# Moving an SSM kernel's skip term from TensorE to GpSimd, and its first loads to two DMA queues

## Chip, cores, metric

One core of one Trainium2 chip. The metric is the device time of one execution in microseconds. The profiled span (first to last instruction) is some 2 us shorter than the time.

## The reference

```python
xn = layernorm(x)                                   # x: 1 x 2048 x 512, bf16
# S5 layer: complex diagonal recurrence over 2048 steps, 512 states
h[t] = Lam_bar * h[t-1] + B_bar @ xn[t]
s = 2 * Re(C @ h) + xn * Dskip                      # the skip term is xn * Dskip
g = silu((gelu(xn @ w_gate) * (xn @ w_up)) @ w_down)    # hidden width 1376
out = x + s * g
```

## The kernel before

It works in four stages of 512 tokens. In each, TensorE does the gated FFN (`ffn`, 11 blocks), the projections for the next stage's scan (`u_pair`), the down projection of four 128-token tiles (`down`) and, in the following stage, the output product of those tiles (`y_mm`). VectorE rotates, scans and rotates back (pp, qq, Wt, Ft, hst), forms the gating products (`at`) and finishes each tile (`epi`). ScalarE empties PSUM (the memory of the tiles that TensorE writes; all these tiles share eight buffers) and applies gelu and silu. `TT` is VectorE's instruction with two inputs, `ACT` one of ScalarE. The skip term costs four small products a tile, of xnT with a diagonal matrix that holds Dskip, accumulated in the same PSUM tile:

```python
def y_mm(s, m, hst):
    ...
    for j in range(2 * NPT):
        nc.tensor.matmul(y_ps[:, :], lhsT=hst[...], rhs=C2[...], start=(j == 0), stop=False)
    for kt in range(KT):                       # the skip term
        nc.tensor.matmul(y_ps[:, kt * P : (kt + 1) * P], lhsT=xnT[:, kt, mg : mg + P],
                         rhs=diagI[:, kt, :], start=False, stop=(kt == KT - 1))

def epi(s, m, y_ps, g2):                       # yg, ot are bf16
    TT(out=yg[:], in0=y_ps[:, :], in1=g2[:], op=ALU.mult)
    TT(out=ot[:], in0=yg[:], in1=x_tok[:, s * M + m, :], op=ALU.add)
```

The loads stand on one queue (sync): four tiles of x, B_re, B_im, then the FFN weights in pieces. The tiny vectors are on the other (scalar). TensorE runs 13 products on zeros while it waits, then transposes B and xn, then starts the first projection.

Of the kernel before, what the change touches and what calls it, by code (L numbers as in the profile page):

```python
# [19 lines left out]
def kernel(  # L20
# [17 lines left out]
    nc = tc.nc  # L38
# [36 lines left out]
    wd = consts.tile([P, NFT, D], BF16, name="wd")  # L75
    BT = consts.tile([P, 2, KT, D], BF16, name="BT")
    C2 = consts.tile([P, 2, NPT, D], BF16, name="C2")
    pv = consts.tile([16, P], BF16, name="pv")
    at0 = work.tile([P, NFT, TS], BF16, name="at", tag="at")
# [7 lines left out]
    wu_r = B_w_up.rearrange("(k p) f -> p k f", p=P)  # L87
    for m in range(M):
        nc.sync.dma_start(out=x_tok[:, m, :], in_=x_r[:, m, :])
    for i, v in enumerate((A_log_dt, A_Lambda_im, A_Lambda_re, A_Dskip)):  # L90
        nc.scalar.dma_start(out=pv[4 * i : 4 * i + 4, :], in_=v.rearrange("(k p) -> k p", p=P))
    for ri, src in enumerate((A_B_re, A_B_im)):
        nc.sync.dma_start(out=Bn[:, ri, :, :], in_=src.rearrange("(k p) d -> p k d", p=P))
    cuts = [0, 3 * P, 7 * P, F]
    for i, (a, b) in enumerate(zip(cuts[:-1], cuts[1:])):
        nc.sync.dma_start(out=wg[:, :, a:b], in_=wg_r[:, :, a:b])
        nc.sync.dma_start(out=wu[:, :, a:b], in_=wu_r[:, :, a:b])
        if i == 0:
            nc.sync.dma_start(out=x_tok[:, M : 2 * M, :], in_=x_r[:, M : 2 * M, :])
# [73 lines left out]

    pf = consts.tile([P, 16], FP32, name="pf")
    ldt, lim, lre, dsk = (pf[:, 4 * i : 4 * i + 4] for i in range(4))
    dt_, thn, a1, rho = (small(n) for n in ("dt_", "thn", "a1", "rho"))
# [6 lines left out]

    dummies(10)
    pt_ps = psum.tile([P, 16], BF16, name="pt_ps", tag="ps")
    nc.tensor.transpose(pt_ps[:, :], pv[:, :], ident[0:16, 0:16])
    dummies(3)
    bn(0, 0)
    bn(0, 1)
    bn_end(0, 0)  # L190
    bn_end(0, 1)
    rstd(0, 0, 2)
    bn(0, 2)
    nc.vector.tensor_copy(out=pf[:], in_=pt_ps[:, :])
    nc.gpsimd.tensor_tensor(out=dt_[:], in0=euler[:], in1=ldt, op=ALU.pow)
    bn(0, 3)
    bn_end(0, 2)
    bn_end(0, 3)
    rstd(0, 2, 4)
    xs = [norm0(0), norm0(1)]  # L200
    STT(out=thn[:], in0=lim, scalar=1.0 / (2.0 * math.pi), in1=dt_[:], op0=ALU.mult, op1=ALU.mult)
    TT(out=a1[:], in0=lre, in1=dt_[:], op=ALU.mult)
    nc.gpsimd.tensor_tensor(out=rho[:], in0=euler[:], in1=a1[:], op=ALU.pow)
    b_transposes(0)
    tps = [t_xn0(0, xs[0]), t_xn0(1, xs[1])]
    xs += [norm0(2), norm0(3)]
    b_transposes(1)
    for m in range(2):
        nc.vector.tensor_copy(out=xnT[:, :, m * P : (m + 1) * P], in_=tps[m][:, :, :])
    tps += [t_xn0(2, xs[2]), t_xn0(3, xs[3])]  # L210
    for m in range(2, 4):
        nc.vector.tensor_copy(out=xnT[:, :, m * P : (m + 1) * P], in_=tps[m][:, :, :])  # L212


# [26 lines left out]
    cre, cim, ncre = small("cre"), small("cim"), small("ncre")  # L241
    diagI = consts.tile([P, KT, P], BF16, name="diagI")

    def coefficients():
# [20 lines left out]
        TSC(out=ncre[:], in0=cre[:], scalar1=-1.0, scalar2=None, op0=ALU.mult)  # L265
        for kt in range(KT):
            TSC(out=diagI[:, kt, :], in0=ident_f[:], scalar1=dsk[:, kt : kt + 1], scalar2=None, op0=ALU.mult)

    def fold_c(pt):
        tA = work.tile([P, D], FP32, name="tA", tag="tA")  # L270
        tB = work.tile([P, D], FP32, name="tB", tag="tB")
        ACT(out=tA[:], in_=CT[:, 1, pt, :], func=AF.Copy, scale=cim[:, pt : pt + 1])
        ACT(out=tB[:], in_=CT[:, 0, pt, :], func=AF.Copy, scale=cim[:, pt : pt + 1])
        dve(now() + 0.8, 0.66, lambda: STT(
            out=C2[:, 0, pt, :], in0=CT[:, 0, pt, :], scalar=cre[:, pt : pt + 1], in1=tA[:],
            op0=ALU.mult, op1=ALU.subtract,
        ))
        dve(now() + 1.6, 0.66, lambda: STT(
            out=C2[:, 1, pt, :], in0=CT[:, 1, pt, :], scalar=ncre[:, pt : pt + 1], in1=tB[:],
            op0=ALU.mult, op1=ALU.subtract,  # L280
        ))
# [151 lines left out]
    def down(s, m, at):  # L433
# [7 lines left out]
        pe_takes(NFT)  # L441
        g2 = work.tile([P, D], FP32, name="g2", tag="g2", bufs=6)
        ACT(out=g2[:], in_=f_ps[:, :], func=AF.Silu)  # L443
        return g2

    def y_mm(s, m, hst):
        m0 = m * P
        mg = s * TS + m0
        for h in range(2):
            flush(("h", s, h))  # L450
        y_ps = psum.tile([P, D], FP32, name="y_ps", tag="ps")
        for j in range(2 * NPT):
            nc.tensor.matmul(  # L453
                y_ps[:, :], lhsT=hst[:, j // NPT, j % NPT, m0 : m0 + P], rhs=C2[:, j // NPT, j % NPT, :],
                start=(j == 0), stop=False,
            )
        for kt in range(KT):
            nc.tensor.matmul(  # L458
                y_ps[:, kt * P : (kt + 1) * P], lhsT=xnT[:, kt, mg : mg + P], rhs=diagI[:, kt, :],
                start=False, stop=(kt == KT - 1),  # L460
            )
        pe_takes(2 * NPT + 1)
        return y_ps

    def epi(s, m, y_ps, g2):
        mg = s * TS + m * P
        yg = work.tile([P, D], BF16, name="yg", tag="yg")
        ot = work.tile([P, D], BF16, name="ot", tag="ot")

        def f():  # L470
            TT(out=yg[:], in0=y_ps[:, :], in1=g2[:], op=ALU.mult)  # L471
            TT(out=ot[:], in0=yg[:], in1=x_tok[:, s * M + m, :], op=ALU.add)

        dve(now() + 0.3, 0.95, f)
        nc.sync.dma_start(out=out_td[mg : mg + P, :], in_=ot[:])

    def y_halves(s, m, hst, g2):
        m0 = m * P
        mg = s * TS + m0
        yg = work.tile([P, D], BF16, name="yg", tag="yg")  # L480
        ot = work.tile([P, D], BF16, name="ot", tag="ot")
        for i in range(2):
            c = slice(i * D // 2, (i + 1) * D // 2)
            y_ps = psum.tile([P, D // 2], FP32, name="y_ps", tag="ps")
            for j in range(2 * NPT):
                nc.tensor.matmul(
                    y_ps[:, :], lhsT=hst[:, j // NPT, j % NPT, m0 : m0 + P], rhs=C2[:, j // NPT, j % NPT, c],
                    start=(j == 0), stop=False,
                )
            for kt in range(KT // 2):  # L490
                k = i * (KT // 2) + kt
                nc.tensor.matmul(
                    y_ps[:, kt * P : (kt + 1) * P], lhsT=xnT[:, k, mg : mg + P], rhs=diagI[:, k, :],
                    start=False, stop=(kt == KT // 2 - 1),
                )
            TT(out=yg[:, c], in0=y_ps[:, :], in1=g2[:, c], op=ALU.mult)
            TT(out=ot[:, c], in0=yg[:, c], in1=x_tok[:, s * M + m, c], op=ALU.add)
            (nc.sync, nc.scalar)[i].dma_start(out=out_td[mg : mg + P, c], in_=ot[:, c])
# [22 lines left out]
    def ln_out(s, m):  # L521
# [3 lines left out]
        nc.sync.dma_start_transpose(out=xnT[:, :, c0 : c0 + P], in_=xn[:])  # L525


    for ri, src in enumerate((A_C_re, A_C_im)):
# [4 lines left out]

    clk["pe"] = 9.5
    clk["dve"] = 11.0
# [91 lines left out]
```

## Time and profile before

| | before |
|---|---|
| time | 189.46 us median of 3 (188.73 to 190.42) |
| span of the profiled run | 187.6 us |
| TensorE, VectorE, GpSimd busy | 96%, 83%, 11% |
| first projection starts | 10.35 us |
| last scan result (hst of stage 3) written | 157.4 us |
| first product on it | 166.6 us |

The busy shares and slices are in the prediction below. Here are two views that it only names. The list of instructions in order of time, TensorE at the start; columns are start (us), length (us), engine, line, operation, output and inputs, shapes, count, and in brackets the idle time before and what ended it:

```profile
6.77 1.07 PE L140 MATMUL tb_ps<-ident,Bn 128*128 128x128 bf16 x16 [1.04 <-DMA Bn<-in_A_B_re_dram]
...
10.35 1.02 PE L333 MATMUL u_ps<-xnT,BT 128*128 128x512 bf16 x4 [0.62 <-DVE xnT L212]
```

TensorE waits 1 us for B_re, then transposes, and starts the real work at 10.35 us. The waits of TensorE over the whole run; columns are who waited for whom, us in total, times, longest:

```profile
PE u_ps L333 <- DVE xnT L212: 0.6, 1, 0.6
PE u_ps L333 <- DMA xnT<-xn: 0.5, 1, 0.5
```

With the 1 us for B_re these are all its waits after the products on zeros. Two groups of VectorE, by form (busy us, mean ns, idle before):

```profile
L382 DVE TENSOR_TENSOR_SCAN Ft<-rho,it,Wt 128x512 bf16<-128x512 f32 x24 | 29.9, 1271 | 0.0
...
L431 DVE TENSOR_TENSOR at<-gt,ub 128x512 bf16<-128x512 bf16 x40 | 16.4, 414 | 5.9 <-ACT ub L430 5.8
```

### The profile page before, as it was taken

The page shows a single profiled execution, that of the slowest core. Times are in us where ns is not written, and L with a number is a line of the kernel's source. Part 1 is how long each engine was busy: PE and PEld are TensorE (multiplying, and loading weights), DVE is VectorE, ACT ScalarE, POOL GpSimd, SP SyncE. Part 2 cuts the span into 40 slices and gives each one's busy share as a digit, 9 for nine tenths or more (in the row PEclk, how much of TensorE's full clock was granted, in tenths as well). Part 3 has the DMA queues.
Part 4 walks back from the last instruction along what each step waited for, and adds up shares of the span by engine and source line. Part 5 has one row for each costly group of instructions (what it writes and reads, how often), then busy time and mean ns, then how long its engine had stood idle before and what let it go on. Part 6 is the DMA issues. An engine that isn't in the chain of part 4 may idle for free.

```text
span 187.6 us, 2592 instructions
## 1 busy us (share of the span) xinstructions
PE 180.8 (96%) x918; PEld 86.0 (46%) x918; DVE 156.0 (83%) x269; ACT 116.2 (62%) x209; POOL 21.2 (11%) x35
## 2 busy tenths in 40 slices
PE   7789999999999999999999999989999999999992
PEld 2644444444444444544444444544444444554452
DVE  4859999999999599999999997999999999332033
ACT  3499899997279969257259947937428733441210
POOL 3745400000000330000000192000000000000000
PEclk9999999999999999999999999999999999999999
DMA  5999968600000013200000001420000000000001
GB/s 145 330 365 361 225 123 246 119 3 0 0 0 0 0 30 86 56 28 28 3 2 0 2 0 42 101 56 28 0 0 0 3 0 28 28 29 31 28 28 58
DMA packets 21164, 12.26 MB, mean 65 GB/s; under 512 B 11456, under 2 KB 21152, under 8 KB 21152
## 3 DMA queue, kind: packets, MB, share of 16 engines
q1 hardware_dynamic: 20976, 12.03, 23.9%
q8 instruction: 7, 0.11, 0.2%
q10 hardware_dynamic: 176, 0.07, 0.1%
q14 instruction: 5, 0.04, 0.1%
HBM read 7.38 MB, written 2.10 MB: 51 GB/s over the span
## 4 chain that ended last, share of the span: by engine, by line
PE 57%; DVE 21%; ACT 10%; DMA 4%; POOL 3%; issue 3%; SPq 1%; POOLq 1%; ACTq 0%; DVEq 0%
PE f_ps L438 15%; PE u_ps L333 11%; PE g_ps L418 10%; PE up_ps L423 10%; PE y_ps L453 6%; DVE Ft L382 6%; ACT junk L508 3%; DVE qq L352 3%; ACT gt L428 3%; ACT ub L430 3%; DVE pp L352 3%; DVE Wt L356 2%; DMA Bn<-in_A_B_re_dram 2%; DMA xnT<-xn 2%; DVE at L431 1%
## 5 line engine op out<-in xcount | busy, mean ns | idle before, releaser
L418 PE MATMUL g_ps<-xnT,wg 128*128 128x512 bf16 (+1 forms) x176 | 45.2, 379 | 0.0
L423 PE MATMUL up_ps<-xnT,wu 128*128 128x512 bf16 (+1 forms) x176 | 45.2, 379 | 0.0
L438 PE MATMUL f_ps<-wd,at 128*128 128x512 bf16 (+1 forms) x176 | 38.7, 379 | 0.0
L428 ACT ACTIVATE gt<-g_ps 128x512 bf16<-128x512 f32 (+1 forms) x44 | 26.0, 592 | 10.0 <-PE g_ps L418 7.8
L382 DVE TENSOR_TENSOR_SCAN Ft<-rho,it,Wt 128x512 bf16<-128x512 f32 x24 | 29.9, 1271 | 0.0
L333 PE MATMUL u_ps<-xnT,BT 128*128 128x512 bf16 x128 | 28.3, 379 | 1.1 <-DVE xnT L212 0.6
L430 ACT ACTIVATE ub<-up_ps 128x512 bf16<-128x512 f32 (+1 forms) x44 | 26.3, 597 | 3.9 <-PE up_ps L423 3.8
L453 PE MATMUL y_ps<-C,hst 128*128 128x512 bf16 x120 | 28.3, 379 | 0.0
L423 PEld LDWEIGHTS <-wu 128*128 128x128 bf16 (+1 forms) x176 | 17.6, 100 | 20.4
L438 PEld LDWEIGHTS <-at 128*128 128x128 bf16 (+1 forms) x176 | 17.2, 98 | 20.6
L443 ACT ACTIVATE g<-f_ps 128x512 f32<-128x512 f32 x16 | 9.6, 597 | 27.1 <-PE f_ps L438 27.1
L418 PEld LDWEIGHTS <-wg 128*128 128x128 bf16 (+1 forms) x176 | 17.2, 100 | 18.4
L431 DVE TENSOR_TENSOR at<-gt,ub 128x512 bf16<-128x512 bf16 (+1 forms) x44 | 18.1, 414 | 7.3 <-ACT ub L430 7.1
L338 ACT ACTIVATE U<-u_ps 128x512 bf16<-128x512 f32 x32 | 17.8, 602 | 9.0 <-PE u_ps L333 9.0
L471 DVE TENSOR_TENSOR yg<-y_ps,g 128x512 bf16<-128x512 f32 x15 | 10.3, 684 | 13.7 <-PE y_ps L458 9.9
L333 PEld LDWEIGHTS <-BT 128*128 128x128 bf16 x128 | 12.3, 98 | 15.9 <-issue 1.4
L453 PEld LDWEIGHTS <-hst 128*128 128x128 bf16 x120 | 11.7, 98 | 13.6
L523 ACT ACTIVATE xn<-x_tok,nb,rs 128x512 bf16<-128x512 bf16 x12 | 9.7, 812 | 5.6 <-POOL nb L519 5.6
L513 POOL TENSOR_SCALAR sx<-sx 128x4 f32<-128x4 f32 x2 | 2.2, 1118 | 82.0 <-ACT junk L508 82.0
L356 DVE TENSOR_TENSOR Wt<-pp,qq 128x1024 bf16<-128x1024 bf16 x16 | 10.6, 688 | 0.3
L356 DVE TENSOR_TENSOR hst<-pp,qq 128x1024 bf16<-128x1024 bf16 x16 | 10.6, 687 | 0.2
L508 ACT ACTIVATE junk<-x_tok 128x512 bf16<-128x512 bf16 x16 | 10.1, 629 | 0.3
(109 smaller groups left out, 163.3 us busy)
## 6 DMA issues: line engine op xcount, KB each, us to landing
out_dram<-ot SPq DMA_DIRECT2D x15, 128.0 KB, 1.7
x_tok<-in_A_x_dram SPq DMA_DIRECT2D x3, 512.0 KB, 3.9
wd<-in_B_w_down_dram SPq DMA_DIRECT2D x1, 1280.0 KB, 10.5
x_tok<-in_A_x_dram SPq DMA_DIRECT2D x4, 128.0 KB, 2.2
Bn<-in_A_B_re_dram SPq DMA_DIRECT2D x1, 512.0 KB
Bn<-in_A_B_im_dram SPq DMA_DIRECT2D x1, 512.0 KB, 5.0
wg<-in_B_w_gate_dram SPq DMA_DIRECT2D x1, 512.0 KB, 9.4
wu<-in_B_w_up_dram SPq DMA_DIRECT2D x1, 512.0 KB
```

Of the source, the lines that this page charges most:

```text
L333: nc.tensor.matmul(u_ps[:, :], lhsT=BT[:, ri, kt, pt * P : (pt + 1) * P], rhs=xnT[:, kt, cols], start=(kt == 0), stop=(kt == KT - 1),)
L338: ACT(out=U[:, ri, q, :], in_=u_ps[:, :], func=AF.Copy)
L356: return lambda: TT(out=dst()[i], in0=box["pp"][:, i, :, :], in1=box["qq"][:, 1 - i, :, :], op=op)
L382: nc.vector.tensor_tensor_scan(out=box["F"][:, ri, q, :], data0=rho[:, pt : pt + 1].to_broadcast([P, TS]), data1=box["W"][:, ri, q, :], in ...
L418: nc.tensor.matmul(g_ps[:fs, :], lhsT=wg[:, kt, fsl], rhs=xnT[:, kt, cols], start=(kt == 0), stop=(kt == KT - 1))
L423: nc.tensor.matmul(u_ps[:fs, :], lhsT=wu[:, kt, fsl], rhs=xnT[:, kt, cols], start=(kt == 0), stop=(kt == KT - 1))
L428: ACT(out=gt[:fs], in_=g_ps[:fs, :], func=AF.Gelu_apprx_tanh)
L430: ACT(out=ub[:fs], in_=u_ps[:fs, :], func=AF.Copy)
L431: dve(now() + 0.9, 0.34, lambda: TT(out=at[:fs, j, :], in0=gt[:fs], in1=ub[:fs], op=ALU.mult))
L438: nc.tensor.matmul(f_ps[:, :], lhsT=at[:fs, k, m0 : m0 + P], rhs=wd[:fs, k, :], start=(k == 0), stop=(k == NFT - 1))
L453: nc.tensor.matmul(y_ps[:, :], lhsT=hst[:, j // NPT, j % NPT, m0 : m0 + P], rhs=C2[:, j // NPT, j % NPT, :], start=(j == 0), stop=False,)
L508: ACT(out=junk[:], in_=x_tok[:, s * M + m, :], func=f, accum_out=sx[:, s, i, m : m + 1])
```

## The change

The intent: take 64 diagonal products off the busiest engine, use the idle GpSimd, keep the sum in fp32, and have x sooner. Cut to its core:

```diff
-    for m in range(M):
-        nc.sync.dma_start(out=x_tok[:, m, :], in_=x_r[:, m, :])
+    nc.sync.dma_start(out=x_tok[:, 0, :], in_=x_r[:, 0, :])
+    nc.scalar.dma_start(out=x_tok[:, 1, :], in_=x_r[:, 1, :])
+    nc.sync.dma_start(out=x_tok[:, 2:M, :], in_=x_r[:, 2:M, :])
+    load_b(nc.sync, 1, A_B_im)
 ... (tiny vectors on scalar; after the second of them:)
+            load_b(nc.scalar, 0, A_B_re)
 ... (order of the first instructions: dummies(12), transposes of B_re first; Db, Dskip copied to every partition, loaded behind the second
     pieces of the FFN weights; for room g2 has 5 buffers instead of 6, and tA and tB share three)
 def down(s, m, at):
     ACT(out=g2[:], in_=f_ps[:, :], func=AF.Silu)
+    xt = x_tok[:, s * M + m, :]
+    r = work.tile([P, D], FP32, name="r", tag="r", bufs=5)
+    nc.gpsimd.tensor_scalar(out=r[:], in0=xt, scalar1=rs[...], scalar2=nb[...], op0=ALU.mult, op1=ALU.add)
+    nc.gpsimd.tensor_tensor(out=r[:], in0=r[:], in1=Db[:], op=ALU.mult)
+    nc.gpsimd.tensor_tensor(out=r[:], in0=r[:], in1=g2[:], op=ALU.mult)
+    nc.gpsimd.tensor_tensor(out=r[:], in0=r[:], in1=xt, op=ALU.add)
 def y_mm(...):
-    for kt in range(KT):
-        nc.tensor.matmul(y_ps[...], lhsT=xnT[...], rhs=diagI[:, kt, :], ...)
 def epi(...):
-    yg = work.tile([P, D], BF16, name="yg", tag="yg")
+    yg = work.tile([P, D], FP32, name="yg", tag="yg")
     TT(out=yg[:], in0=y_ps[:, :], in1=g2[:], op=ALU.mult)
-    TT(out=ot[:], in0=yg[:], in1=x_tok[:, s * M + m, :], op=ALU.add)
+    TT(out=ot[:], in0=yg[:], in1=r[:], op=ALU.add)
```

More of the change, by code (lines that the diff above doesn't have):

```diff
@@ L76 @@
     BT = consts.tile([P, 2, KT, D], BF16, name="BT")
+    Db = consts.tile([P, D], BF16, name="Db")
     C2 = consts.tile([P, 2, NPT, D], BF16, name="C2")
-    pv = consts.tile([16, P], BF16, name="pv")
+    pv = consts.tile([12, P], BF16, name="pv")
     at0 = work.tile([P, NFT, TS], BF16, name="at", tag="at")
@@ L87, with load_b @@
     wu_r = B_w_up.rearrange("(k p) f -> p k f", p=P)
-    for m in range(M):
-        nc.sync.dma_start(out=x_tok[:, m, :], in_=x_r[:, m, :])
-    for i, v in enumerate((A_log_dt, A_Lambda_im, A_Lambda_re, A_Dskip)):
+    def load_b(eng, ri, src):
+        eng.dma_start(out=Bn[:, ri, :, :], in_=src.rearrange("(k p) d -> p k d", p=P))
+    nc.sync.dma_start(out=x_tok[:, 0, :], in_=x_r[:, 0, :])
+    nc.scalar.dma_start(out=x_tok[:, 1, :], in_=x_r[:, 1, :])
+    nc.sync.dma_start(out=x_tok[:, 2:M, :], in_=x_r[:, 2:M, :])
+    load_b(nc.sync, 1, A_B_im)
+    for i, v in enumerate((A_log_dt, A_Lambda_im, A_Lambda_re)):
         nc.scalar.dma_start(out=pv[4 * i : 4 * i + 4, :], in_=v.rearrange("(k p) -> k p", p=P))
-    for ri, src in enumerate((A_B_re, A_B_im)):
-        nc.sync.dma_start(out=Bn[:, ri, :, :], in_=src.rearrange("(k p) d -> p k d", p=P))
+        if i == 1:
+            load_b(nc.scalar, 0, A_B_re)
     cuts = [0, 3 * P, 7 * P, F]
@@ L97 @@
         nc.sync.dma_start(out=wu[:, :, a:b], in_=wu_r[:, :, a:b])
+        if i == 1:
+            nc.sync.dma_start(out=Db[:], in_=A_Dskip.unsqueeze(0).to_broadcast([P, D]))
         if i == 0:
@@ L172, in t_xn0 @@
         return tp
-    pf = consts.tile([P, 16], FP32, name="pf")
-    ldt, lim, lre, dsk = (pf[:, 4 * i : 4 * i + 4] for i in range(4))
+    pf = consts.tile([P, 12], FP32, name="pf")
+    ldt, lim, lre = (pf[:, 4 * i : 4 * i + 4] for i in range(3))
     dt_, thn, a1, rho = (small(n) for n in ("dt_", "thn", "a1", "rho"))
@@ L181 @@
     ch = consts.tile(W3, BF16, name="ch")
-    dummies(10)
-    pt_ps = psum.tile([P, 16], BF16, name="pt_ps", tag="ps")
-    nc.tensor.transpose(pt_ps[:, :], pv[:, :], ident[0:16, 0:16])
-    dummies(3)
-    bn(0, 0)
-    bn(0, 1)
-    bn_end(0, 0)
-    bn_end(0, 1)
-    rstd(0, 0, 2)
-    bn(0, 2)
+    dummies(12)
+    b_transposes(0)
+    for a in (0, 2):
+        for m in (a, a + 1):
+            bn(0, m)
+        for m in (a, a + 1):
+            bn_end(0, m)
+        rstd(0, a, a + 2)
+    xs = [norm0(0), norm0(1)]
+    tps = [t_xn0(0, xs[0]), t_xn0(1, xs[1])]
+    pt_ps = psum.tile([P, 12], BF16, name="pt_ps", tag="ps")
+    nc.tensor.transpose(pt_ps[:, :], pv[:, :], ident[0:12, 0:12])
+    b_transposes(1)
     nc.vector.tensor_copy(out=pf[:], in_=pt_ps[:, :])
     nc.gpsimd.tensor_tensor(out=dt_[:], in0=euler[:], in1=ldt, op=ALU.pow)
-    bn(0, 3)
-    bn_end(0, 2)
-    bn_end(0, 3)
-    rstd(0, 2, 4)
-    xs = [norm0(0), norm0(1)]
-    STT(out=thn[:], in0=lim, scalar=1.0 / (2.0 * math.pi), in1=dt_[:], op0=ALU.mult, op1=ALU.mult)
-    TT(out=a1[:], in0=lre, in1=dt_[:], op=ALU.mult)
-    nc.gpsimd.tensor_tensor(out=rho[:], in0=euler[:], in1=a1[:], op=ALU.pow)
-    b_transposes(0)
-    tps = [t_xn0(0, xs[0]), t_xn0(1, xs[1])]
     xs += [norm0(2), norm0(3)]
-    b_transposes(1)
     for m in range(2):
@@ L212 @@
         nc.vector.tensor_copy(out=xnT[:, :, m * P : (m + 1) * P], in_=tps[m][:, :, :])
+    STT(out=thn[:], in0=lim, scalar=1.0 / (2.0 * math.pi), in1=dt_[:], op0=ALU.mult, op1=ALU.mult)
+    TT(out=a1[:], in0=lre, in1=dt_[:], op=ALU.mult)
+    nc.gpsimd.tensor_tensor(out=rho[:], in0=euler[:], in1=a1[:], op=ALU.pow)
     TT(out=ang[:], in0=iota_f[:].unsqueeze(1).to_broadcast(W3), in1=thn[:].unsqueeze(2).to_broadcast(W3), op=ALU.mult)
@@ L241 @@
     cre, cim, ncre = small("cre"), small("cim"), small("ncre")
-    diagI = consts.tile([P, KT, P], BF16, name="diagI")
     def coefficients():
@@ L265, in coefficients @@
         TSC(out=ncre[:], in0=cre[:], scalar1=-1.0, scalar2=None, op0=ALU.mult)
-        for kt in range(KT):
-            TSC(out=diagI[:, kt, :], in0=ident_f[:], scalar1=dsk[:, kt : kt + 1], scalar2=None, op0=ALU.mult)
     def fold_c(pt):
-        tA = work.tile([P, D], FP32, name="tA", tag="tA")
-        tB = work.tile([P, D], FP32, name="tB", tag="tB")
+        tA = work.tile([P, D], FP32, name="tA", tag="tt", bufs=3)
+        tB = work.tile([P, D], FP32, name="tB", tag="tt", bufs=3)
         ACT(out=tA[:], in_=CT[:, 1, pt, :], func=AF.Copy, scale=cim[:, pt : pt + 1])
@@ L441, in down @@
         pe_takes(NFT)
-        g2 = work.tile([P, D], FP32, name="g2", tag="g2", bufs=6)
+        g2 = work.tile([P, D], FP32, name="g2", tag="g2", bufs=5)
         ACT(out=g2[:], in_=f_ps[:, :], func=AF.Silu)
-        return g2
+        xt = x_tok[:, s * M + m, :]
+        r = work.tile([P, D], FP32, name="r", tag="r", bufs=5)
+        nc.gpsimd.tensor_scalar(
+            out=r[:], in0=xt, scalar1=rs[:, s, m : m + 1], scalar2=nb[:, s, m : m + 1], op0=ALU.mult, op1=ALU.add
+        )
+        nc.gpsimd.tensor_tensor(out=r[:], in0=r[:], in1=Db[:], op=ALU.mult)
+        nc.gpsimd.tensor_tensor(out=r[:], in0=r[:], in1=g2[:], op=ALU.mult)
+        nc.gpsimd.tensor_tensor(out=r[:], in0=r[:], in1=xt, op=ALU.add)
+        return g2, r
     def y_mm(s, m, hst):
@@ L454, in y_mm @@
                 y_ps[:, :], lhsT=hst[:, j // NPT, j % NPT, m0 : m0 + P], rhs=C2[:, j // NPT, j % NPT, :],
-                start=(j == 0), stop=False,
+                start=(j == 0), stop=(j == 2 * NPT - 1),
             )
-        for kt in range(KT):
-            nc.tensor.matmul(
-                y_ps[:, kt * P : (kt + 1) * P], lhsT=xnT[:, kt, mg : mg + P], rhs=diagI[:, kt, :],
-                start=False, stop=(kt == KT - 1),
-            )
-        pe_takes(2 * NPT + 1)
+        pe_takes(2 * NPT)
         return y_ps
@@ L466, in epi @@
         mg = s * TS + m * P
-        yg = work.tile([P, D], BF16, name="yg", tag="yg")
+        yg = work.tile([P, D], FP32, name="yg", tag="yg")
+        g2, r = g2
         ot = work.tile([P, D], BF16, name="ot", tag="ot")
@@ L471, in f @@
             TT(out=yg[:], in0=y_ps[:, :], in1=g2[:], op=ALU.mult)
-            TT(out=ot[:], in0=yg[:], in1=x_tok[:, s * M + m, :], op=ALU.add)
-        dve(now() + 0.3, 0.95, f)
+            TT(out=ot[:], in0=yg[:], in1=r[:], op=ALU.add)
+        dve(now() + 0.3, 1.2, f)
         nc.sync.dma_start(out=out_td[mg : mg + P, :], in_=ot[:])
@@ L479, in y_halves @@
         mg = s * TS + m0
-        yg = work.tile([P, D], BF16, name="yg", tag="yg")
+        yg = work.tile([P, D], FP32, name="yg", tag="yg")
+        g2, r = g2
         ot = work.tile([P, D], BF16, name="ot", tag="ot")
@@ L487, in y_halves @@
                     y_ps[:, :], lhsT=hst[:, j // NPT, j % NPT, m0 : m0 + P], rhs=C2[:, j // NPT, j % NPT, c],
-                    start=(j == 0), stop=False,
-                )
-            for kt in range(KT // 2):
-                k = i * (KT // 2) + kt
-                nc.tensor.matmul(
-                    y_ps[:, kt * P : (kt + 1) * P], lhsT=xnT[:, k, mg : mg + P], rhs=diagI[:, k, :],
-                    start=False, stop=(kt == KT // 2 - 1),
+                    start=(j == 0), stop=(j == 2 * NPT - 1),
                 )
             TT(out=yg[:, c], in0=y_ps[:, :], in1=g2[:, c], op=ALU.mult)
-            TT(out=ot[:, c], in0=yg[:, c], in1=x_tok[:, s * M + m, c], op=ALU.add)
+            TT(out=ot[:, c], in0=yg[:, c], in1=r[:, c], op=ALU.add)
             (nc.sync, nc.scalar)[i].dma_start(out=out_td[mg : mg + P, c], in_=ot[:, c])
@@ L525, in ln_out @@
         nc.sync.dma_start_transpose(out=xnT[:, :, c0 : c0 + P], in_=xn[:])
+    nc.gpsimd.tensor_tensor(out=nb[:, 0, :], in0=mv[:, 0, :, 0], in1=rs[:, 0, :], op=ALU.mult)
+    nc.gpsimd.tensor_scalar(out=nb[:, 0, :], in0=nb[:, 0, :], scalar1=-1.0, scalar2=None, op0=ALU.mult)
     for ri, src in enumerate((A_C_re, A_C_im)):
@@ L532 @@
         nc.sync.dma_start(out=x_tok[:, s * M : (s + 1) * M, :], in_=x_r[:, s * M : (s + 1) * M, :])
-    clk["pe"] = 9.5
+    clk["pe"] = 9.3
     clk["dve"] = 11.0
```

## The prediction

> **What bounds the kernel now.** I read the page first (busy shares, the 40 slices), then the waits, then the list of instructions in order of time for GpSimd (POOL) and VectorE (DVE) around three places: the start, the LayerNorm statistics near 107 us, and the end. Busy shares and slices:
>
> ```profile
> PE 180.8 (96%) x918; PEld 86.0 (46%) x918; DVE 156.0 (83%) x269; ACT 116.2 (62%) x209; POOL 21.2 (11%) x35
> ...
> PE   7789999999999999999999999989999999999992
> PEld 2644444444444444544444444544444444554452
> DVE  4859999999999599999999997999999999332033
> ```
>
> TensorE has no gap from 10.35 us, where the first projection starts, to 184.1 us. In the table of waits PE waits only 1.1 us before its large products after warm-up (0.6 for the first xnT, 0.5 for the xnT of the last stage). So it is the bound, and what is taken off it can come off the time, as long as nothing else is close behind. But VectorE is close behind: it has nines in nearly every slice from the fourth to the thirty-fourth. The windows view gives DVE 15.91 of 16.6 us busy from 36.4 to 53.0, 24.05 of 26.5 to 79.5, 17.19 of 17.5 to 97.0, 24.91 of 26.4 to 123.4, 16.29 of 16.6 to 140.0. Between 36.4 and 157.4 us, where the last scan stage's hst is written, I count some 5.6 us of idle VectorE. The only other reserve is that this hst is first read at 166.6 us, 9.2 us later.
>
> What the change removes and touches, from the groups by form:
>
> ```profile
> L458 PE MATMUL y_ps<-diagI,xnT 128*128 128x128 bf16 x60 | 5.8, 219 | 0.0
> ...
> L471 DVE TENSOR_TENSOR yg<-y_ps,g 128x512 bf16<-128x512 f32 x15 | 10.3, 684 | 13.7 <-PE y_ps L458 9.9 <-ACT g L443 3.8
> L352 DVE TENSOR_TENSOR pp<-U,cos_b 128x2048 bf16<-128x2048 bf16 x8 | 9.8, 1222 | 0.4
> L472 DVE TENSOR_TENSOR ot<-yg,x_tok 128x512 bf16<-128x512 bf16 x15 | 6.4, 425 | 0.5
> L236 POOL COPY sa<-sh 128x2048 bf16<-128x2048 bf16 x1 | 1.9, 1892 | 3.5 <-ACT sh L219 3.5
> ```
>
> The mean of 219 ns is the latency of one pipelined product. What four of them occupy is seen in the chain that ended last: "PE y_ps L458 x4" takes 0.22 us.
>
> The lines that decide my prediction are GpSimd's seven tiny instructions (4 numbers per partition) at 107 us, and the same at 63 us, beside VectorE's in order of time. First GpSimd, then VectorE:
>
> ```profile
> 63.62 0.98 POOL L513 TENSOR_SCALAR sx<-sx 128x4 f32<-128x4 f32 x1 [42.54 <-ACT junk L508]
> 64.69 0.20 POOL L514 TENSOR_TENSOR mq<-sx 128x4 f32<-128x4 f32 x1
> ...
> 107.13 1.25 POOL L513 TENSOR_SCALAR sx<-sx 128x4 f32<-128x4 f32 x1 [39.45 <-ACT junk L508]
> 108.46 0.62 POOL L514 TENSOR_TENSOR mq<-sx 128x4 f32<-128x4 f32 x1
> ```
> ```profile
> 63.30 1.22 DVE L352 TENSOR_TENSOR pp<-U,cos_b 128x2048 bf16<-128x2048 bf16 x1
> ...
> 107.08 1.22 DVE L352 TENSOR_TENSOR qq<-Ft,sin_b 128x2048 bf16<-128x2048 bf16 x1
> 108.33 0.69 DVE L356 TENSOR_TENSOR hst<-pp,qq 128x1024 bf16<-128x1024 bf16 x1
> ```
>
> The same L514 takes 0.20 us where VectorE is idle (64.52 to 65.30) and 0.62 us beside a VectorE product. Each GpSimd instruction that starts beside a two-input VectorE instruction ends 0.05 to 0.09 us after that one: 64.60 after 64.52, 108.38 after 108.30, 109.08 after 109.02. So GpSimd is held until VectorE's instruction is over. Whether a long GpSimd instruction holds VectorE the same way this trace cannot show: the one long one, the copy of 1.89 us, ran while VectorE was idle or read one operand.
>
> **What the Trainium skill says.** "SBUF — State Buffer", Who interferes with whom: VectorE's second port is GpSimd's only one; a VectorE instruction with two SBUF inputs and a GpSimd instruction that reads SBUF exclude each other, for the whole instruction of whichever started first. The trace agrees in the one direction it shows. "GPSIMD Engine Reference", Elementwise — side-by-side cycle accounting: a two-input fp32 instruction of 2048 elements took 4497 ns, or about 2.2 ns an element; no run here has one yet. "TensorE: Matmul & The Clock Gate", Wait — 56ns, not 53.3ns?: 55.6 ns from start to start at 128 columns; the trace's 0.22 us for four agrees. "VectorE: DVE Perf Modes", What auto-detection actually checks: two results a cycle only if every tensor is 16-bit. The trace agrees: 425 ns for the all-bf16 add of 512, against 684 ns for the product that reads fp32.
>
> **The change part by part.**
> (1) TensorE. 64 diagonal products go: 16 tiles x 0.22 us = 3.5 us, all on the bound. Four in five of them lie before the last tiles, so this would be visible at the end only if nothing else takes over.
> (2) VectorE. The add becomes fp32: 425 to about 690 ns, so 0.26 us x 16 = 4.2 us more. The product stays at 684 ns, since its inputs were fp32 already. Four diagonal builds of 281 ns go (1.1 us). Net +3.1 us on an engine with 5.6 + 9.2 us of reserve: alone, bearable. At the end, where one add of 0.43 and two half adds of 0.29 us follow the last products, some 0.3 to 0.5 us become visible.
> (3) GpSimd. Four instructions for each of 16 tiles. Estimates: the affine step reads one input, at the copy's 1892/2048 = 0.92 ns an element 0.5 us; the three two-input steps at the skill's 2.2 ns an element 1.1 us each, in all 3.9 to 4.0 us a tile, 63 us for the kernel. GpSimd's own time suffices (21 us busy now), so by its own sum it is no bound.
> (4) The port. Of VectorE's work in a stage of 43.2 us, nearly all has two SBUF inputs: the rotations, combinations, scans and gating products. Only the yg products (0.68 us, one input in PSUM) and statistics are free of it. Twelve of the 16 tiles have their GpSimd work inside the crowded stretch 43 to 157 us; the last four fall after the last scans. If GpSimd holds the port for its whole 4.0 us a tile, that is 48 us. Off this go the idle 5.6 us and ten yg products of 0.68 us: 48 - 12.4 = 35.6 us of stall for VectorE. With the ten slower adds in the stretch (2.6 us), hst is ready at 157.4 + 35.6 + 2.6 = 195.6 us. From the first product on this hst to the end it is 187.6 - 166.6 = 21.0 us now, 20.5 us after (four times 0.22 less, slower adds at the end). Span 216, and with the 1.9 us by which time exceeds the span, 218 us. If the port is held only while operands are read (estimate: one operand element a cycle at 1.2 GHz, the clock given in "GPSIMD Engine Reference", so 0.43 + 3 x 0.85 = 3.0 us a tile), it is 36 - 12.4 = 23.6 us of stall, hst at 183.6, span 204, time 206 us.
> (5) Order on GpSimd. The skip work of four tiles stands before the next stage's LayerNorm statistics in GpSimd's queue. These were just in time before (PE waited 0.5 us for the last stage's xnT), so a queue that is 5 to 10 us late makes TensorE wait even where VectorE does not.
> (6) Start. Two x tiles go over two queues, B_re no longer waits behind four x issues. The first B tile was awaited until 6.72 us; some 0.3 us earlier at the first projection, since bandwidth is shared and the chain of transposes and copies stays.
> (7) End. After the silu of the last stage's first tile (171.7 us), GpSimd has two steps of that tile and twelve of the others left, 14 to 15 us; the last is ready near 186, where the add read its operand at 183.8 before. About 2 us, if not hidden by (4).
>
> **The rivals.** A, the port is exclusive both ways and VectorE becomes the bound: 203 to 218 us. For it: GpSimd's stretched instructions, VectorE's nines, the skill. Against it: no lengthened VectorE instruction is seen, but GpSimd's were tiny and their reads fit between two VectorE instructions. B, GpSimd only ever waits, VectorE runs on: then its burst of 16 instructions takes 22 us or more instead of 16, statistics come late by 6 to 9 us in two stages, TensorE's 3.5 us are spent there: 189 to 195 us. C, the intended: all hidden, 189.5 - 3.5 - 0.3 + 0.5 + 1 (the wait for xnT that opens when TensorE is earlier) = 187 us. Against C speaks that it needs both a free port and a punctual GpSimd.
>
> **Range and chances.** I give A some three chances in four, with its middle at 206 to 208 us, and B and C the rest. The point is a little under A's middle: 205 us. The range 188 to 217 us reaches down into C and nearly up to the full lock. Faster by over 2% (under 185.7) needs C and a better start: 0.08. Within 2% (to 193.2) is C or a mild B: 0.14. Slower: 0.78.
>
> **What would show it.** (1) is right if the y products are 64 fewer at the same pace. (2) if the add takes near 690 ns. (3) if GpSimd's steps, where VectorE is idle (at the end), take about 0.5 and 1.1 us. (4) is right if VectorE's two-input instructions (pp, qq, scans, at) show means well above 1222, 1271 and 414 ns, or gaps before them, just where GpSimd runs, and if TensorE gets gaps with gating products or hst as releaser. If these means are unchanged and TensorE has no gaps, A is wrong and the time is under 190. (5) shows as a wait of PE for xnT of several us. The prediction is wrong above all if a GpSimd instruction gives the port back between its elements, or takes much less than 1.1 us.

## The result

233.82 us median of 4 (233.71 to 234.15) against 189.14 us in the same rounds: ratio 1.2351, 95% interval 1.2288 to 1.2415. A ratio here is the mean time of one kernel's runs over that of the other's of the same rounds, so it is not quite the ratio of the medians. Executions over 1.5% slower than the fastest of the same kernel are left out of the means. The direction was foreseen, the size was not: the time lies above the range.

The page of the changed kernel, busy shares and slices (40 equal parts of 232.0 us, busy tenths; PEclk is TensorE's granted clock in tenths):

```profile
PE 188.5 (81%) x837; PEld 86.1 (37%) x853; DVE 198.0 (85%) x265; ACT 116.7 (50%) x209; POOL 123.4 (53%) x101
...
PE   7489999999970799999997739499999931999920
...
DVE  4289799899999999999999999999999999942232
...
POOL 3158400029999920009999980001999990006993
PEclk9889999999996599999999976979999995699985
```

TensorE now has three deep holes (about 64 to 81, 122 to 139 and 186 to 197 us), each in the second half of a burst of nines in GpSimd's row or just behind it, with a lower clock in or after each. VectorE has nines without a break from the ninth slice to the thirty-fifth. From 36.4 to 200.0 us the windows view gives it 160.9 of 163.6 us busy: it is the bound there. It did not get that much more work: 198.0 - 156.0 = 42.0 us more busy time, of which the adds explain 4.8 (15 x 0.30 and two halves of 0.13), less 1.1 for the diagonal builds. Some 38.3 us are left. The groups show where they are:

```profile
L382 DVE TENSOR_TENSOR_SCAN Ft<-rho,it,Wt 128x512 bf16<-128x512 f32 x24 | 37.7, 1589 | 0.0
...
L431 DVE TENSOR_TENSOR at<-gt,ub 128x512 bf16<-128x512 bf16 x40 | 23.1, 582 | 2.1 <-ACT ub L430 2.0
...
L352 DVE TENSOR_TENSOR pp<-U,cos_b 128x2048 bf16<-128x2048 bf16 x8 | 11.4, 1426 | 0.3
L477 DVE TENSOR_TENSOR ot<-yg,r 128x512 bf16<-128x512 f32 x15 | 10.9, 724 | 5.0 <-POOL r L452 3.7
...
L447 POOL TENSOR_SCALAR r<-x_tok,rs,nb 128x512 f32<-128x512 bf16 x16 | 26.7, 1666 | 0.0
...
L451 POOL TENSOR_TENSOR r<-r,g 128x512 f32<-128x512 f32 x16 | 28.1, 1756 | 89.2 <-ACT g L443 88.3
```

Instructions that did not change at all are longer: the scans 1589 ns instead of 1271, the gating products 582 instead of 414. GpSimd's own steps are long too: 1666 and 1756 ns in the mean, 0.77 and 1.27 us where VectorE is idle. How the two hold each other is seen in order of time, first GpSimd, then VectorE, around 72 us:

```profile
70.20 1.34 POOL L450 TENSOR_TENSOR r<-r,Db 128x512 f32<-128x512 f32 x1
71.62 2.13 POOL L451 TENSOR_TENSOR r<-r,g 128x512 f32<-128x512 f32 x1
73.83 1.21 POOL L452 TENSOR_TENSOR r<-r,x_tok 128x512 f32<-128x512 f32 x1
```
```profile
70.45 2.17 DVE L352 TENSOR_TENSOR pp<-Ft,cos_b 128x2048 bf16<-128x2048 bf16 x1
...
72.55 1.48 DVE L431 TENSOR_TENSOR at<-gt,ub 128x512 bf16<-128x512 bf16 x1
73.95 2.17 DVE L352 TENSOR_TENSOR qq<-Ft,sin_b 128x2048 bf16<-128x2048 bf16 x1
```

They take turns. GpSimd's L450 begins at 70.20; pp, 1.22 us of work, ends only at 72.62, as if it had begun at 71.40, shortly before L450's end. GpSimd's L451, 1.27 us alone, then ends at 73.75, 1.13 us after pp. The gating product, 0.42 us of work, ends at 74.03 and so takes 1.48. Each of the three VectorE instructions, qq too, is about 1 us longer.

TensorE's waits now, the large ones:

```profile
PE y_ps L462 <- DVE hst L356: 8.7, 1, 8.7
PE g_ps L418 <- DVE yg L476: 8.4, 1, 8.4
PE g_ps L418 <- ACT gt L428: 5.4, 3, 4.8
...
PE u_ps L333 <- DMA xnT<-xn: 3.1, 1, 3.1
```

The first two wait for VectorE itself; in the second, g_ps needs a PSUM buffer, and the one that comes free is that of a y_ps, once the product yg has read it. The third is ScalarE, which mostly waited in its turn for the gating products. The fourth is the statistics behind GpSimd's burst. Two places outside the middle also changed. The start, TensorE in order of time:

```profile
9.68 1.82 PE L148 MATMUL tb_ps<-ident,Bn 128*128 128x128 bf16 x16 [3.20 <-DMA Bn<-in_A_B_re_dram]
...
14.90 3.40 PE L333 MATMUL u_ps<-xnT,BT 128*128 128x512 bf16 x14 [0.62 <-DVE xnT L212]
```

B_re arrives 2.9 us later, the sixteen transposes take 1.82 instead of 1.07 us, and the first projection starts 4.55 us later. And the end, GpSimd from the last stage's first silu to its last step:

```profile
210.53 1.27 POOL L451 TENSOR_TENSOR r<-r,g 128x512 f32<-128x512 f32 x1 [18.91 <-ACT g L443]
...
226.98 1.15 POOL L452 TENSOR_TENSOR r<-r,x_tok 128x512 f32<-128x512 f32 x1
```

TensorE is done at 222.1 us; the last adds wait for GpSimd until 228.1 us.

### The profile page after: what moved, and what is told of

Same layout as the page of the kernel before. It is cut to its first block, busy times and chain, and to the rows that moved or that the text cites. A ratio compares the mean times of both kernels' runs of the same rounds, so it can differ in the third digit from the quotient of the medians.

```text
span 232.0 us, 2527 instructions
## 1 busy us (share of the span) xinstructions
PE 188.5 (81%) x837; PEld 86.1 (37%) x853; DVE 198.0 (85%) x265; ACT 116.7 (50%) x209; POOL 123.4 (53%) x101
## 5 line engine op out<-in xcount | busy, mean ns | idle before, releaser
L451 POOL TENSOR_TENSOR r<-r,g 128x512 f32<-128x512 f32 x16 | 28.1, 1756 | 89.2 <-ACT g L443 88.3
L418 PE MATMUL g_ps<-xnT,wg 128*128 128x512 bf16 (+1 forms) x174 | 47.5, 396 | 14.1 <-DVE yg L476 8.4
L462 PE MATMUL y_ps<-C,hst 128*128 128x512 bf16 x114 | 30.5, 409 | 8.9 <-DVE hst L356 8.7
L382 DVE TENSOR_TENSOR_SCAN Ft<-rho,it,Wt 128x512 bf16<-128x512 f32 x24 | 37.7, 1589 | 0.0
L431 DVE TENSOR_TENSOR at<-gt,ub 128x512 bf16<-128x512 bf16 (+1 forms) x44 | 24.8, 567 | 3.2 <-ACT ub L430 2.9
L447 POOL TENSOR_SCALAR r<-x_tok,rs,nb 128x512 f32<-128x512 bf16 x16 | 26.7, 1666 | 0.0
L452 POOL TENSOR_TENSOR r<-r,x_tok 128x512 f32<-128x512 f32 x16 | 24.8, 1550 | 1.3
L450 POOL TENSOR_TENSOR r<-r,Db 128x512 f32<-128x512 f32 x16 | 23.2, 1453 | 1.3
L476 DVE TENSOR_TENSOR yg<-y_ps,g 128x512 f32<-128x512 f32 x15 | 10.2, 681 | 9.0 <-PE y_ps L462 5.6
L356 DVE TENSOR_TENSOR Wt<-pp,qq 128x1024 bf16<-128x1024 bf16 x16 | 17.2, 1100 | 0.2
```

Source lines behind the costliest of these rows:

```text
L382: nc.vector.tensor_tensor_scan(out=box["F"][:, ri, q, :], data0=rho[:, pt : pt + 1].to_broadcast([P, TS]), data1=box["W"][:, ri, q, :], in ...
L418: nc.tensor.matmul(g_ps[:fs, :], lhsT=wg[:, kt, fsl], rhs=xnT[:, kt, cols], start=(kt == 0), stop=(kt == KT - 1))
L447: nc.gpsimd.tensor_scalar(out=r[:], in0=xt, scalar1=rs[:, s, m : m + 1], scalar2=nb[:, s, m : m + 1], op0=ALU.mult, op1=ALU.add)
L450: nc.gpsimd.tensor_tensor(out=r[:], in0=r[:], in1=Db[:], op=ALU.mult)
L451: nc.gpsimd.tensor_tensor(out=r[:], in0=r[:], in1=g2[:], op=ALU.mult)
L452: nc.gpsimd.tensor_tensor(out=r[:], in0=r[:], in1=xt, op=ALU.add)
```

## The experiments

Fifteen runs. **A** is the theory that VectorE and GpSimd exclude each other at the port of SBUF (the memory in which their tiles lie), the start and the end being separate costs.

### Do the parts add? start_only, skip_only

start_only is the kernel before with the new list of loads and the new order of the first instructions, nothing else:

```diff
 # the kernel before
-    (loads and first instructions of before)
+    (loads and first instructions of the changed kernel, Dskip still in pv)
```

> The kernel before with only the new start (x over both DMA queues, B_re on the second queue, the new order of the first instructions; the diagonal products stay). In the changed kernel the first projection begins at 14.90 us instead of 10.35, because B_re lands at 9.68 us instead of 6.77. Theory A (start and skip term are separate costs that add): time 189.1 + 4.5 = 193 to 194.5 us, first projection near 14.9 us. Rival (the late start of the changed kernel comes from the broadcast load of D or from anything on GpSimd): first projection near 10.3 us, time 189 us.

skip_only is the changed kernel with the opposite edit:

```diff
 # the changed kernel
-    (its loads and first instructions)
+    (loads and first instructions of before; Dskip's broadcast load stays)
```

> The changed kernel with the start of the kernel before: skip term on GpSimd, diagonal products gone. Theory A (the shared port costs VectorE about 34 us in the middle, GpSimd's last tiles another 5 us at the end): 233.8 - 4.5 = 228 to 230.5 us. Rival (a late start shifts the scans against the gating products and so makes the rest slow): clearly under 225 us.

Measured in the same rounds, before at 189.44: start_only 193.10 us (ratio 1.021, interval 1.0172 to 1.0249), first projection at 14.92 us; skip_only 230.24 us (ratio 1.2169, interval 1.2130 to 1.2207). 3.7 + 40.8 = 44.5 us; the whole change cost 233.82 - 189.14 = 44.7. The parts add, and neither D's load nor GpSimd has to do with the start. As skip_only starts at 10.38 us like before, it can be laid beside it:

| us, profiled runs | before | skip_only | difference |
|---|---|---|---|
| last hst written | 157.4 | 194.8 | +37.4 |
| from there to its first product | 9.2 | 6.4 | -2.8 |
| from there to the end of the span | 21.0 | 26.6 | +5.6 |

### The parts that were meant to matter: diag_off, add_fp32

```diff
 # diag_off: the kernel before (wrong result on purpose: the skip term is missing)
-        for kt in range(KT):
-            nc.tensor.matmul(y_ps[...], lhsT=xnT[...], rhs=diagI[:, kt, :], ...)
```

> The kernel before without its 64 diagonal products and with nothing in their place (wrong result on purpose, the skip term is missing): what the change could gain at most. If every one of the 3.5 us lies on the path that sets the end: 185.6 us. I expect that the wait for the last stage's xnT takes back the share of the first eight tiles (1.8 us), since VectorE and ScalarE and with them the statistics do not come sooner: 186.5 to 187.5 us.

```diff
 # add_fp32: the kernel before
-        yg = work.tile([P, D], BF16, name="yg", tag="yg")
+        yg = work.tile([P, D], FP32, name="yg", tag="yg")
```

> The kernel before with yg in fp32, so that the last add has an fp32 operand; nothing else changed. The add should take near 690 ns instead of 425, 4.2 us more VectorE work. Theory A (VectorE has 5.6 us idle and 9.2 us of slack): at most 1.5 us at the end and at the xnT of the last stage, 189.3 to 190.8 us. Rival (VectorE is so full that fp32 itself is what made the changed kernel slow): 193 us or more.

Measured: diag_off 186.42 us (ratio 0.9847, 0.9818 to 0.9876), so some 3.0 us are all that there was to gain (the first projection of its profiled run came 1.35 us later than before, at 11.70, without an edit there). The wait for the last stage's xnT did not open, as I had expected: that run shows none. add_fp32 189.90 us (ratio 1.0034, 1.0004 to 1.0064): the fp32 add is not the cause.

### Is it the port, GpSimd's slowness, or its queue? pool_two, pool_one, pool_write

The kernel before, diagonal products included, with useless work behind each silu on tiles that nobody reads:

```diff
         ACT(out=g2[:], in_=f_ps[:, :], func=AF.Silu)
+        nc.gpsimd.tensor_copy(out=pt_[:], in_=g2[:, 0:1])     # starts it at the same moment
+        for _ in range(4):
+            nc.gpsimd.tensor_tensor(out=po[:], in0=pa[:], in1=pa[:], op=ALU.mult)      # pool_two
+          # nc.gpsimd.tensor_scalar(out=po[:], in0=pa[:], scalar1=2.0, scalar2=1.0, ...)  # pool_one
+          # nc.gpsimd.memset(po[:], 0.0)                          # pool_write, 1280 elements
```

> The kernel before, diagonal products and all, with useless work added on GpSimd: after each silu a one-element read of its result and then four two-input fp32 multiplications of 512 elements, on tiles that nobody else uses. Nothing waits for them but the LayerNorm statistics behind them in GpSimd's queue. Theory A (each GpSimd read holds VectorE off the shared port): about 0.95 us of VectorE for each of the 48 in the crowded stretch, less some 12 us of idle time and one-input instructions, so 215 to 228 us, and VectorE's two-input groups (scans, combinations, gating products) with means 30 to 60% longer. Rival (GpSimd is only slow, and lateness of what it produces costs the time): under 196 us, VectorE's means unchanged.

> As the last, but four one-input fp32 affine steps of 512 elements (alone near 0.8 us each). Theory A: they hold the port for the shorter time that they read (0.45 to 0.7 us), so about half to three quarters of the loss of the two-input version: 202 to 218 us. If only two-input GpSimd instructions excluded VectorE: under 194 us.

> As the last two, but four fills of 1280 fp32 elements, which write and read nothing; I guess from the fill of 128 elements in 0.20 us that they take near 1.1 us each. Theory A as the Trainium skill has it (only reads exclude a two-input VectorE instruction): VectorE's means unchanged, and only the statistics 2 to 3 us later: 189 to 193 us. Rival (any work on GpSimd slows VectorE): as the two-input version, over 210 us. Rival (GpSimd's queue being late): the same few us in all three.

Measured, before at 189.64 us: pool_two 226.66 us (ratio 1.1957), pool_one 202.38 us (1.0676), pool_write 197.53 us (1.0420). The scans and GpSimd's work in the groups by form, pool_two, pool_one and pool_write in turn:

```profile
L386 DVE TENSOR_TENSOR_SCAN Ft<-rho,it,Wt 128x512 bf16<-128x512 f32 x24 | 35.2, 1492 | 0.0
...
L450 POOL TENSOR_TENSOR po<-pa 128x512 f32<-128x512 f32 x64 | 89.8, 1403 | 3.8
```
```profile
L386 DVE TENSOR_TENSOR_SCAN Ft<-rho,it,Wt 128x512 bf16<-128x512 f32 x24 | 32.7, 1384 | 0.0
...
L450 POOL TENSOR_SCALAR po<-pa 128x512 f32<-128x512 f32 x64 | 64.0, 1000 | 4.0
```
```profile
L384 DVE TENSOR_TENSOR_SCAN Ft<-rho,it,Wt 128x512 bf16<-128x512 f32 x24 | 29.9, 1272 | 0.0
...
L448 POOL MEMSET po<- 128x1280 f32 x64 | 74.5, 1164 | 2.8
```

The fills keep GpSimd longer than the one-input steps do (74.5 us against 64.0), and yet the scan's mean is 1272 ns as in the kernel before; VectorE's total is 156.3 us against 156.0. With reads it is 173.8 and 196.2 us. So it is reading by GpSimd that lengthens VectorE's instructions, not activity on GpSimd, and this alone, with no part of the change present, makes up most of the loss: of pool_two's 37 us only some 2.5 are useless work that runs on after the output, since its last add ends at 220.56 us against 184.90. Spread over the 48 instructions in the crowded stretch (the last 16 run where VectorE is mostly idle), a two-input step costs VectorE at most (196.2 - 156.0)/48 = 0.84 us and a one-input step 17.8/48 = 0.37 us. Both are less than the shortest of these instructions lasts (1.04 and 0.61 us). As an estimate, the change's three two-input steps and one one-input step come to at most 3 x 0.84 + 0.37 = 2.9 us a tile by this; the changed kernel lost 38.3 us in 12 tiles, or 3.2.

Two of my expectations were too high. In pool_two the means of VectorE's two-input groups grew by 17% (the scans) to 52% (hst), not by 30 to 60%. And pool_one lost a third of what pool_two did (12.7 of 37.0 us), not half to three quarters.

pool_write was 4 to 5 us above what I expected, though its VectorE instructions are not longer. Its last add ends at 187.80 us against 184.90, of which 0.67 is a later first projection (11.02); the remaining 2.2 us fit the late statistics (not shown by a run of their own), for which ScalarE's xn waits 11.4 us in all instead of 5.6. The rest of its span, to 195.1, is the useless fills themselves, which run on after the output.

### Middle or end? skip_0to2

```diff
 # the kernel before, with the GpSimd steps of the change where s < 3
+    SK = (0, 1, 2)      # y_mm: diagonal products only if s not in SK; epi: r instead of x_tok if s in SK
```

> The start of the kernel before; skip term on GpSimd for the first three stages as in the changed kernel (yg kept in bf16 for room), diagonal products for the last stage. Theory A (middle and end are separate costs): the loss of the middle stays, the one at the end goes: 230.2 - 5.5 = 223.5 to 226 us. Rival (GpSimd's lateness at the end is the larger part): under 215 us.

Measured: 223.82 us (ratio 1.1785, 1.1714 to 1.1857). The last stage's GpSimd work costs 230.24 - 223.82 = 6.4 us; the first three stages cost the other 34.

### The start: start_swap, start_sp, dma_only, order_only, start_warm

```diff
 # start_swap: start_only
-    load_b(nc.sync, 1, A_B_im)   ...   load_b(nc.scalar, 0, A_B_re)
+    load_b(nc.sync, 0, A_B_re)   ...   load_b(nc.scalar, 1, A_B_im)
```

> start_only with the two B loads exchanged between the queues: B_re third on the first queue, B_im on the second. Theory S (a load on the second queue gets a small share beside the first queue's long row of loads, whichever load it is): B_re lands near 5.7 us, B_im near 9 us, the second group of transposes waits for it, time about as start_only, 192 to 194 us. Rival (B_re itself, or the new order of the first instructions, is what is slow): B_im lands by 7.5 us.

```diff
 # start_sp: the kernel before, only x spread over the queues
-    for m in range(M):
-        nc.sync.dma_start(out=x_tok[:, m, :], in_=x_r[:, m, :])
+    (tile 0 on sync, tile 1 on scalar, tiles 2 and 3 on sync; B_re, B_im stay on sync)
```

> The kernel before with x alone spread over both queues (tile 0 and tiles 2 and 3 together on the first, tile 1 on the second); B_re and B_im stay on the first queue, now third and fourth, and the order of instructions is that of before. Theory S: B_re is issued 1 us earlier and lands up to 1 us earlier, the first projection begins 0.3 to 0.8 us earlier, time 0.3 to 0.8 us less, 188.7 to 189.2 us. Rival (spreading x itself delays): 189.5 us or more.

Measured: start_swap 191.87 us (ratio 1.0147). B_re, now on the first queue, was issued at 1.64 us and still landed 7.1 us later, so my theory of a small share for the second queue fell; so did its rival, for B_im landed near 10.2 us and not by 7.5. start_sp 189.17 us (ratio 1.0012, 0.9973 to 1.0050): B_re landed 4.8 us after its issue and the first projection began at 10.40 us. Spreading x does no harm and no good. What remained open was tried with three more runs:

> The kernel before with only the new list of loads; instructions in the order of before. If the loads are the cause: B_re lands near 9 us as in start_only, first projection at 13.5 to 15 us, time 192 to 194 us. If the order of instructions is: near 10.4 us and 189 us.

> The kernel before with only the new order of the first instructions; loads as before. If the loads are the cause: first projection at 10.3 to 11 us, 189 to 190 us. If the order is: 12 us or more.

```diff
 # start_warm: start_only
-    dummies(12)
+    dummies(26)
```

> start_only with 26 instead of 12 warming products, so that TensorE works until about 9 us, when B_re lands: the transposes should take 1.07 us for sixteen again instead of 1.89. If the low clock after the gap is a part of the cost, the first projection begins 1.5 to 2 us sooner than the 14.9 us of start_only, time 191 to 192 us. If not, 14.9 us and 193 us.

dma_only (the new loads alone): 193.89 us, two runs 2.7 us apart (ratio 1.0206, 0.9997 to 1.0416), first projection at 14.25 us. order_only (the new order alone): 189.29 us (ratio 0.9964), first projection at 10.95 us, inside the 10.35 to 11.70 us that the runs with the start of before show. So it is the loads. start_warm: 192.29 us (ratio 1.0122, 0.9979 to 1.0265; by time alone it can't be told from start_only's 1.021), first projection at 12.75 us. The transposes in order of time, start_only and start_warm:

```profile
8.90 1.89 PE L145 MATMUL tb_ps<-ident,Bn 128*128 128x128 bf16 x16 [3.58 <-DMA Bn<-in_A_B_re_dram]
```
```profile
8.89 1.07 PE L145 MATMUL tb_ps<-ident,Bn 128*128 128x128 bf16 x16 [0.60 <-DMA Bn<-in_A_B_re_dram]
```

With B_re at the same moment, work on zeros during the wait brings the first projection from 14.92 to 12.75 us. In start_only the granted clock is 0.50 from 8 to 10 us, after the wait of 3.6 us; in start_warm, with a wait of 0.6 us, it is 1.00. So of the 4.6 us lost at the start 2.2 are TensorE's low clock, and 2.1 are B_re's lateness (8.90 against 6.77 us), by one profiled run each.

Why B_re is late, start_swap and start_sp narrow down. Both issue it on the first queue at the same moment (1.64 and 1.67 us), and it lands 7.1 and 4.8 us later. Beside it start_swap issues B_im at 2.08 us and the first FFN weights at 2.15, start_sp not before 3.60 and 4.01. (The other difference is the order of instructions, which order_only cleared.) The bytes fit: by the GB/s of each microsecond, 1.4 MB had moved when it landed at 6.77 us in the kernel before, 2.5 MB when it landed at 9.68 us in the changed one, while the first four tiles of x and B_re are 1.0 MB. There B_im and the first FFN weights were issued at 1.64 and 2.15 us, around B_re's 2.08. How the engines divide themselves among loads in flight was not taken apart.

### A version with the good parts: skip_3_early, both_small

GpSimd only in the last stage, when the scans are over, with the steps that need x alone done for all four tiles before the silus:

```diff
 # skip_3_early: the kernel before with SK = (3,); both_small: the same with start_sp's loads
+    nc.gpsimd.tensor_copy(out=gate[:], in_=ats[s][:, 8, 0:1])   # not before this gating product
+    for m in range(M):
+        skip_a(s, m)          # affine step and product with D
```

> The kernel before with the skip term on GpSimd for the last stage alone, where VectorE's scans are over: the two steps that need only x are done for all four tiles before the silus, behind a read of a late gating product; the two others after each silu. Diagonal products stay in stages 0 to 2. Theory A (exclusion costs only where VectorE is full, lateness at the end only because the x steps stood between the others): no loss, 4 x 0.22 us of TensorE gained, 0.3 to 0.4 us given back to the fp32 adds at the end: 188.6 to 189.4 us. Rival (GpSimd at the end is too slow in any order): 191 us or more.

> start_sp and skip_3_early together: if the two gains add, 188.2 to 188.9 us, 0.3 to 0.6% under the kernel before. If neither holds, 189.4 us.

Measured: 189.78 us (ratio 1.0041, 1.0006 to 1.0075) and 190.15 us (1.0061, 1.0028 to 1.0095), against 189.13 us. The big loss is gone, which bears A out: GpSimd does four tiles where VectorE is mostly idle and the time stays within 0.6%. But nothing is won. VectorE's last fp32 adds take part of it: from the end of the last full tile's products to the last add it is 3.2 us here (181.31 to 184.54) against 2.75 us before (182.15 to 184.90). Even so that last add ends 0.4 us earlier than before, though the first projection came 0.6 us later (10.91). What is lost in the profiled run lies behind it: from the last add to the end of the span it is 3.3 us, in both_small 3.2, against 2.7 before. Why was not tried. No correct version here beats the kernel before by more than the noise. These two runs also have the fewer buffers for g2, tA and tB, so those cost the changed kernel 1% at most.

## Why the prediction was wrong

By its own steps:

**(1) TensorE** was right: 3.5 us of work, 3.0 visible (diag_off). (The stretch that I called without a gap has one of 0.5 us, the wait for xnT that I list beside it.) **(2) VectorE** was right: the add has a median of 693 ns (690 foreseen), and the cost by itself is 0.3% (add_fp32). **(3) GpSimd's own time** was a little low. Alone the steps take 0.77, 1.16, 1.27 and 1.15 us, with gaps 4.7 us a tile instead of 4.0.

**(4) The port**: mechanism right, shown by the three pool runs. Each of its two terms was mis-sized. VectorE lost 38.3/12 = 3.2 us a tile: near the 3.0 us of "held only while operands are read", not the 4.0 us of the whole instruction. The deduction of 12.4 us hardly existed. VectorE's idle time from the first projection to the last hst fell only from 7.6 us (of 147.1) to 4.9 us (of 184.8). The sum over the stretch hid that GpSimd's work stands in three bursts (51.0 to 75.0, 104.5 to 130.6, 161.7 to 191.6 us, 80.1 us together). Here they are by the windows view; columns are the window, its length, and each engine's busy time (instructions), then the granted clock, the DMA share and GB/s:

```profile
51.02:75.04 24.02, 17.10 (x79) 7.57 (x78) 23.85 (x19) 14.40 (x32) 23.22 (x15) 0.92 0.00 0
104.48:130.60 26.12, 23.95 (x110) 10.74 (x111) 25.88 (x21) 14.40 (x32) 25.32 (x15) 1.00 0.01 2
161.68:191.60 29.92, 25.51 (x115) 11.37 (x117) 29.71 (x22) 11.68 (x20) 29.04 (x16) 0.98 0.00 1
```

In them VectorE, the third engine of the row, is idle for 0.6 us, and not one yg product, which I let run beside GpSimd's work, falls into them: the first after each is at 83.7, 139.7 and 195.6 us. The two errors cancel in the full-lock version, which by luck has hst at 195.6 us (194.8 measured in skip_only). In the read-only version, toward which I pulled the point, only the second error remains, and it has 183.6.

**From hst to the end**, the step that the prediction did not work out: it let TensorE stand ready when hst comes, and 20.5 us follow. In skip_only 6.4 us pass first, since TensorE's own FFN blocks were held up by VectorE's work queued behind the scans (the wait of 8.4 us for yg above, which skip_only has too). Then 26.6 us follow instead of 20.5. **(7) The end** was taken as about 2 us if not hidden. After the first silu of the last stage GpSimd needs 17.6 us for 14 steps (210.53 to 228.13), while TensorE is done within 11.6 us of it; the last stage's share is 6.4 us (skip_0to2).

**(6) The start** had the wrong sign: 0.3 us gain foreseen, 3.7 us loss (start_only). I looked at the moment of issue and not at what else is in flight, and had no term for the clock after a gap.

**(5) The queue order** is real and small: TensorE waits 3.1 us for xnT, and pool_write shows 2.2 us from it, less than the 6 to 9 that rival B had.

**Range**: A's own upper case was 218 us and lay outside the range. From the read-only version's span of 204.1 us to the 232.0 measured, 11.2 us are hst's lateness (194.8 against 183.6), 6.4 pass until its first product, 6.1 are after it (26.6 against 20.5), and 4.2 come with the start (the spans grew by 44.4 and 40.2 us with and without it): 27.9 us. These are parts of the runs' own spans, so they say where the time went and test nothing by themselves. The low clock in the middle (0.91 from 36.4 to 200 us) goes with TensorE's gaps. That gaps bring it was tried at the start alone; no run took it away in the middle, but VectorE is busy 98% of that stretch.

## What to carry to other kernels

An engine at 11% is not free if its work must read SBUF while a full VectorE reads two operands from it: count the held time as VectorE's work, burst by burst, and take nothing off for idle time that lies elsewhere. Work that only writes did not lengthen VectorE's instructions, and a place where VectorE is mostly idle cost under 1%, though neither gained anything here. The load that the first product waits for wants as little as possible in flight beside it, whatever queue it is on.

## What the Trainium skill lacked or had wrong

- "SBUF — State Buffer", SBUF: two separate sides, says that whichever instruction starts first has the shared port for its whole length. Here VectorE lost at most 0.84 us per two-input GpSimd instruction of at least 1.04 us, and 0.37 us per one-input instruction of at least 0.61 us, so counting the whole length overstates the loss. For how long the port itself is held no run shows. That GpSimd instructions which only write do not contend with VectorE's two-input ones is as the page says, under Who interferes with whom (1272 ns against 1271).
- "GPSIMD Engine Reference", Engine selection, calls one-input steps roughly line rate; at that page's 1.2 GHz, 512 elements would be an estimated 0.43 us. An fp32 affine step took at least 0.61 us. A step of 4 elements takes 0.20 us here, so the difference is about as large as a fixed part, for which the page gives no figure.
- "Trainium Kernel Development and Optimization", Key Constraints, says that loads of all queues interleave on the same engines and that issuing from several only saves issue time. It lacks that the time saved can cost, when it puts other loads in flight beside the one that is awaited: B_re landed 7.6 us after its issue instead of 4.1, and the first projection came up to 4.6 us later. It was not the second queue itself: on the first, B_re took 7.1 us in start_swap.
